# Retention attention and a Strassen feed-forward block in float32: weight rounding dealt out step by step, two evictions on ScalarE, sums of x^T kept in DRAM, a denser start

## The chip, the cores and the metric

The kernel runs on one core of a Trainium2 chip. The time is device microseconds of one execution, and the kernel before took 1169.26 us (median of 3 runs, 1168.03 to 1170.57). Five engines work from queues of their own, each in order: TensorE (PE in the profile, its weight loads PEld), VectorE (DVE), ScalarE (ACT), GpSimd (POOL) and SyncE (SP), which here issues nearly all DMAs. An instruction whose input isn't ready holds up everything behind it on its engine.

## The reference

```python
scores = scale * np.matmul(q, k.transpose(0, 1, 3, 2))          # q, k, v: (8, 8, 576, 64) float32
Dmat = np.where(rel >= 0, gamma[:, None, None] ** rel[None, :, :], 0.0)
attn = np.matmul(scores * Dmat[None], v)                        # no softmax: a decay per head instead
x = np.ascontiguousarray(attn.transpose(0, 2, 1, 3)).reshape(B * S, H * D)     # (4608, 512)
h = x @ w_in                                                    # w_in (512, 2048), float64
sp = np.maximum(h, 0.0) + np.log1p(np.exp(-np.abs(h)))
out = (h * erf(sp)) @ w_out                                     # w_out (2048, 512), float64
```

The weights come as float64; the kernel reads both 32-bit words of each and builds a float32 from them itself.

## The kernel before, in words

**Work units.** The 4608 tokens are cut into 9 chunks of 512 columns of x^T, and the 2048 columns of w_in into 4 groups g of 512. A slice n = 9g + c is one group on one chunk; there are 36. Each slice has a `First` (h = x w_in, then softplus and erf) and a `Second` (the product with w_out, added to an output sum o). Each is one level of Strassen's scheme in Winograd's form: seven products in place of eight. First n computes A11 A12 | S2 S3 S1 | S4 A22 (`first`, `middle`, `last`), Second n computes B11 B21 | T2 T3 T1 | B22 T4. One product is four float32 matmuls of 128x128x256; the trace shows each of them as two, so a product is a row "x8". All products of one half add into the same PSUM tile `a` one after the other (the partial sums): before the next product may add to it, the present sum must have been copied out. `t` (t1, t2) holds h, `s` its softplus, erf and sums, `g` and `e` are two further PSUM tiles, which First and Second share.

**Sums.** Strassen needs sums of the left and right operands. Those of the weights are made once for each group, four for `wa` (w_in) and four for `wb` (w_out), by `sums_in` and `sums_out` (L150, L156). Those of x^T are made for each slice by `sums_x` (L351) on VectorE into a tile `xs`: 4 sums for each of the 36 slices. Chunk c of x^T is written to DRAM (`xd`, 1 MB) when attention has made it, and read back by `load_x` for groups 1 to 3.

**Rounding.** A group has 8 weight parts, four of `wa` and four of `wb`, 512 KB each, in the raw tiles `wraw`. `round_weights` (L173) does one whole part at a call: two instructions on ScalarE, four on VectorE (L191, L194, L197, L201), two on GpSimd (L202, L203), then the load of the part four further on, and after the fourth part of `wa` or `wb` the four sums. It is called at seven places in the start, once behind First 0 and then once at the end of each Second (L566), so that a fourth part comes in every fourth slice.

**Attention** goes in 40 pieces of 128 (or 64) tokens, each in stages `transposes`, `scores`, `outputs`. The stages of chunk 0 come first; those of later chunks are dealt out one behind each product of group 0 (`run`, `attend`). `transposes(i)` also starts the loads of piece i+2 (three raw buffers).

**Order.** The program is written out by hand in the loop at L543: First n: S2 S3 S1, then Second n-1: B11 B21, First n: S4 A22, Second n-1: T2 T3 T1, First n+1: A11 A12, Second n-1: B22 T4, and so on. Each engine runs its instructions in that order. Behind S2 and S1, VectorE copies the partial sum out (L396, L401); behind A11 and S4 ScalarE does (L386, L407). At L545 to L548 the output sum o of Second n-1 (1 MB, `od`) and x^T of slice n+1 are loaded; in the last slice but one, o's load stands behind the stores (L573).

Of the kernel before, what the change touches and what calls it, by code (L numbers as in the profile page):

```python
# [11 lines left out]
FP32 = mybir.dt.float32  # L12
UINT8 = mybir.dt.uint8
UINT32 = mybir.dt.uint32
# [4 lines left out]
P = 128  # L19
# [27 lines left out]
def kernel(  # L47
# [69 lines left out]
    gk = gk.rearrange("p (s h) -> p s h", s=NS)  # L117
    gq = gq.rearrange("p (a i) -> p a i", a=NP)
    load(1)

# [26 lines left out]

    def sums_in(a11, s3, a12, a22, s1, s2, s4):  # L150
        tt(s1, s3, a22, ALU.add)
        tt(s2, s1, a11, ALU.subtract)
        tt(s3, a11, s3, ALU.subtract)
        tt(s4, a12, s2, ALU.subtract)

    def sums_out(b11, t3, b21, b22, t1, t2, t4):  # L156
        tt(t1, t3, b11, ALU.subtract)
        tt(t2, b22, t1, ALU.subtract)
        tt(t3, b22, t3, ALU.subtract)
        tt(t4, b21, t2, ALU.subtract)  # L160

    coming = parts()
    words = []
    rounded = [0]

    def load_weights():
        part = next(coming, None)
# [2 lines left out]
            nc.sync.dma_start(out=t[:, :].rearrange("p (h f) -> p h f", h=2), in_=part[0])  # L170
            words.append((t, *part[1:]))

    def round_weights():  # L173


        if not words:
            return
        t, name, g, slot, j, sums = words.pop(0)
        rounded[0] += 1
        w = operands(name, g)  # L180
        dst = w[:, slot : slot + 2, j, :]
        pairs = t[:, :].rearrange("p (h f two) -> p h f two", h=2, two=2)
        pairs_f = t[:, :].bitcast(FP32).rearrange("p (h f two) -> p h f two", h=2, two=2)
        low, high = pairs[:, :, :, 0], pairs[:, :, :, 1]
        r_f, high_f = pairs_f[:, :, :, 0], pairs_f[:, :, :, 1]
        a_f, a = dst, dst.bitcast(UINT32)
        nc.scalar.activation(a_f, high_f, AF.Abs)
        nc.scalar.mul(out=r_f, in_=low, mul=2.0**-52)


        nc.vector.tensor_scalar(  # L191
            out=a_f, in0=a_f, scalar1=HIGH_LEAST, scalar2=HIGH_MOST, op0=ALU.max, op1=ALU.min
        )
        nc.vector.tensor_scalar(  # L194
            out=a, in0=a, scalar1=3, scalar2=0x3FFFFFFF, op0=ALU.logical_shift_left, op1=ALU.bitwise_and
        )
        nc.vector.scalar_tensor_tensor(  # L197
            out=a, in0=high, scalar=0xC0000000, in1=a, op0=ALU.bitwise_and, op1=ALU.bitwise_or
        )

        nc.vector.tensor_scalar(out=high, in0=a, scalar1=0xFF800000, scalar2=None, op0=ALU.bitwise_and)  # L201
        nc.gpsimd.tensor_tensor(out=r_f, in0=high_f, in1=r_f, op=ALU.mult)  # L202
        nc.gpsimd.tensor_tensor(out=a_f, in0=a_f, in1=r_f, op=ALU.add)  # L203
        load_weights()
        if sums:
            sums(*(w[:, i] for i in range(7)))

    for _ in range(4):
        load_weights()

    ident = cpool.tile([P, P], FP32, name="ident")
    make_identity(nc, ident)
# [3 lines left out]
        nc.vector.memset(t, 0.0)  # L216


    x = {}
    live = {}  # L220
    kept = {}

# [37 lines left out]
    def outputs(i):  # L260
# [44 lines left out]
        while t0 < b * S + s0 + n:  # L305
            c = t0 // TCH
            if (0, c) not in x:
                x[0, c] = xpool.tile([P, n_dc, TCH], FP32, tag="x", name="x")
# [13 lines left out]
            t0 += m  # L322
            if t0 == (c + 1) * TCH:
                nc.sync.dma_start(out=xd[c], in_=x[0, c])

    stages = [(transposes, 0), (scores, 0)]
    for i in range(len(pieces)):
# [17 lines left out]


    def load_x(g, c):
        x[g, c] = xpool.tile([P, n_dc, TCH], FP32, tag="x", name="x")
        nc.sync.dma_start(out=x[g, c], in_=xd[c])

    def sums_x(g, c):  # L351
        t = x[g, c]
        s = xpool.tile([P, 4, 2, TH], FP32, tag="xs", name="xs")
        b11, b12, b21, b22 = (t[:, 2 * d : 2 * d + 2, h * TH : (h + 1) * TH] for d in range(2) for h in range(2))
        t1, t2, t3, t4 = (s[:, j] for j in range(4))
        tt(t1, b12, b11, ALU.subtract)
        tt(t2, b22, t1, ALU.subtract)
        tt(t3, b22, b12, ALU.subtract)
        tt(t4, b21, t2, ALU.subtract)
        x[g, c] = {A11: b11, A12: b21, S4: b22, A22: t4, S1: t1, S2: t2, S3: t3}  # L360

    class First:

# [40 lines left out]

# [122 lines left out]
    sums_x(0, 0)  # L527

    def run(steps):

        for _ in steps:
            attend(done[0] + 1)

    run(firsts[0].first())
    run(firsts[0].middle())
    run(firsts[0].last())
    firsts[0].erf()
    round_weights()
    attend(stages_for(2 * TCH))
    sums_x(0, 1)  # L540
    run(firsts[1].first())
    firsts[0].multiply()
    for b, nxt in zip(blocks[1:], blocks[2:] + [None]):  # L543
        n = order.index((b.g, b.c))
        if isinstance(b, First):  # L545
            seconds[n - 1].begin()
            if n + 1 < n_s and order[n + 1][0] > 0:
                load_x(*order[n + 1])  # L548
            run(b.middle())
            firsts[n - 1].sums()  # L550
            run(seconds[n - 1].first())
            run(b.last())
        elif n + 2 < n_s:
            f = firsts[n + 1]
            steps = b.middle()
            for step, _ in enumerate(steps):
                attend(done[0] + 1)
# [4 lines left out]
            sums_x(*order[n + 2])  # L562
            run(nxt.first())
            f.multiply()
            run(b.last())
            round_weights()  # L566
        elif n + 1 < n_s:
            firsts[n + 1].erf()
            run(b.middle())
            run(b.last())  # L570
            firsts[n + 1].multiply()
            firsts[n + 1].sums()
            seconds[n + 1].begin()  # L573
            run(nxt.first())
        else:
            run(b.middle())
            run(b.last())
# [30 lines left out]
```

## Time and profile before

| | |
|---|---|
| median of 3 runs | 1169.26 us |
| the profiled execution | 1166.91 us, its span 1165.1 us |
| busy: PE, DVE, ACT, POOL | 1082.6, 736.1, 372.1, 120.0 us |
| DMA | 150.27 MB, 40.2% of 16 engines |
| mean granted TensorE clock | 0.974 of 2.4 GHz |

TensorE is busy for 93% of the span, and the other engines for less than two thirds. What matters is what stands in the gaps of TensorE, and how the clock goes behind them. A time of an instruction is its start from the beginning of the span; "[5.11 <-DVE t L396]" behind a row says that its engine stood idle for 5.11 us before it, and which instruction ended the wait.

### The profile page before, as it was taken

How to read it: one execution, taken by the hardware profiler on the slowest of the kernel's cores; microseconds unless marked ns; L12 is line 12 of the kernel's file. 1: busy time of each engine (PE TensorE's matmuls, PEld its weight loads, DVE VectorE, ACT ScalarE, POOL GpSimd, SP SyncE). 2: the span in 40 equal slices, each digit the busy share in tenths (PEclk: the TensorE clock that was granted, in tenths of full speed). 3: DMA queues.
4: the chain of work that ended last, by engine and by line, in shares of the span. 5: the costliest groups of instructions: out<-in, count | busy, mean ns of one | idle time of the engine just before them, and what ended most of it. 6: DMA issues, size and time to landing. Idle time of an engine off the chain costs nothing. (4 is left out here: it accounts for less than half of the span.)

```text
span 1165.1 us, 15647 instructions
## 1 busy us (share of the span) xinstructions
PE 1082.6 (93%) x6400; PEld 922.7 (79%) x6400; DVE 736.1 (63%) x1240; ACT 372.1 (32%) x467; POOL 120.0 (10%) x110
## 2 busy tenths in 40 slices
PE   6679999999999998998999799989998999999996
PEld 5457888888788887876878688868887888888885
DVE  5756566666576575766566566666775565665654
ACT  3231433424314233333333333424332224322340
POOL 3411111111111000011000000000000000000000
PEclk8888999999999999999999899999999999999998
DMA  9546454554554122343234424332232442234422
GB/s 229 143 128 137 100 137 136 132 136 134 139 127 114 73 91 91 132 158 153 100 136 151 158 105 173 127 126 109 109 136 80 167 159 109 109 113 167 154 73 108
DMA packets 141127, 150.27 MB, mean 129 GB/s; under 512 B 115200, under 2 KB 115200, under 8 KB 132992
## 3 DMA queue, kind: packets, MB, share of 16 engines
q1 hardware_dynamic: 140912, 148.92, 40.2%
q8 instruction: 50, 0.82, 0.3%
q10 hardware_dynamic: 144, 0.36, 0.1%
q14 instruction: 21, 0.17, 0.0%
HBM read 102.07 MB, written 47.19 MB: 128 GB/s over the span
## 5 line engine op out<-in xcount | busy, mean ns | idle before, releaser
L450 PE MATMUL a<-wb,s 128*128 128x256 f32 x864 | 208.1, 384 | 10.8 <-DVE o L91 10.8
L450 PEld LDWEIGHTS a<-wb,s 128*128 128x128 f32 x864 | 162.7, 191 | 37.2 <-DVE o L91 12.6
L371 PE MATMUL a<-xs,wa 128*128 128x256 f32 x576 | 147.4, 401 | 32.9 <-DVE t L396 31.4
L407 ACT COPY t<-a 128x512 f32<-128x512 f32 x36 | 21.1, 585 | 435.3 <-PE a L371 420.4
L91 DVE TENSOR_TENSOR o<-a,o 128x512 f32<-128x512 f32 x108 | 74.4, 689 | 134.8 <-PE a L450 104.2
L371 PEld LDWEIGHTS a<-xs,wa 128*128 128x128 f32 x576 | 112.0, 199 | 56.1 <-DVE t L396 38.6
L371 PE MATMUL a<-x,wa 128*128 128x256 f32 x576 | 137.3, 381 | 0.0
L371 PE MATMUL g<-xs,wa 128*128 128x256 f32 x576 | 137.1, 381 | 0.0
L371 PEld LDWEIGHTS g<-xs,wa 128*128 128x128 f32 x576 | 108.2, 190 | 14.9
L371 PEld LDWEIGHTS a<-x,wa 128*128 128x128 f32 x576 | 108.1, 190 | 15.0
L202 POOL TENSOR_TENSOR wraw<-wraw 128x512 f32<-128x512 f32 x32 | 34.9, 1090 | 530.0 <-issue 425.6
L91 DVE TENSOR_TENSOR t<-t,s 128x1024 f32<-128x1024 f32 x72 | 85.9, 1234 | 0.0
L413 ACT ACTIVATE s<-t 128x1024 f32<-128x1024 f32 x72 | 72.1, 1048 | 36.1 <-DVE t L91 36.1
L91 DVE TENSOR_TENSOR t<-g,t 128x512 f32<-128x512 f32 x72 | 49.7, 690 | 43.9 <-PE g L371 42.6
L401 DVE COPY t<-a 128x512 f32<-128x512 f32 x36 | 24.9, 690 | 79.9 <-PE a L371 79.9
L418 ACT ACTIVATE s<-s 128x1024 f32<-128x1024 f32 x72 | 72.1, 1049 | 0.4
L450 PE MATMUL a<-wb,t 128*128 128x256 f32 x288 | 70.3, 388 | 1.9 <-DVE t L91 1.9
L371 PE MATMUL e<-x,wa 128*128 128x256 f32 x288 | 68.8, 382 | 0.0
L450 PE MATMUL g<-wb,s 128*128 128x256 f32 x288 | 68.6, 381 | 0.0
L450 PE MATMUL g<-wb,t 128*128 128x256 f32 x288 | 68.6, 381 | 0.0
L450 PE MATMUL e<-wb,t 128*128 128x256 f32 x288 | 68.4, 380 | 0.0
L228 POOL TENSOR_TENSOR raw_v<-raw_v,cst 128x512 f32<-128x512 f32 (+1 forms) x40 | 43.3, 1082 | 223.3 <-DMA raw_v<-in_v_dram 210.9
(61 smaller groups left out, 1435.3 us busy)
## 6 DMA issues: line engine op xcount, KB each, us to landing
od<-o SPq DMA_DIRECT2D x54, 512.0 KB, 3.1
x<-xd SPq DMA_DIRECT2D x27, 1024.0 KB, 8.9
o<-od SPq DMA_DIRECT2D x27, 1024.0 KB, 7.1
xd<-x SPq DMA_DIRECT2D x9, 1024.0 KB, 5.2
out_dram<-o SPq DMA_DIRECT2D x18, 512.0 KB, 3.0
raw_q<-in_q_dram SPq DMA_DIRECT2D x32, 256.0 KB, 4.8
raw_k<-in_k_dram SPq DMA_DIRECT2D x32, 256.0 KB, 3.9
raw_v<-in_v_dram SPq DMA_DIRECT2D x32, 256.0 KB, 4.0
```

The source lines that it names most:

```text
L91: nc.vector.tensor_tensor(out=out, in0=in0, in1=in1, op=op)
L202: nc.gpsimd.tensor_tensor(out=r_f, in0=high_f, in1=r_f, op=ALU.mult)
L228: nc.gpsimd.tensor_tensor(out=t[:n], in0=t[:n], in1=gk[:n, s0 // P, :].unsqueeze(2).to_broadcast([n, H, D]), op=ALU.mult,)
L371: nc.tensor.matmul(acc[:, j * TH : (j + 1) * TH], lhsT=weights["wa", self.g][:, a, d, j * P : (j + 1) * P], rhs=x[self.g, self.c][a][:, d, :],
L401: nc.vector.tensor_copy(out=self.t2[:, 1], in_=self.a)
L407: nc.scalar.copy(out=self.t2[:, 0], in_=self.a)
L413: nc.scalar.activation(self.s[:, j], t, AF.Softplus)
L418: nc.scalar.activation(self.s[:, j], self.s[:, j], AF.Erf)
L450: nc.tensor.matmul(acc[:, tp, :], lhsT=left[:, j * TH + tp * P : j * TH + (tp + 1) * P], rhs=weights["wb", self.g][:, b, j, :], start=(sta ...
```

## The change

`rounding` is now a generator that yields behind each step: the two ScalarE instructions, each of the first three VectorE instructions, the fourth with the GpSimd pair and the next load, and each sum of the weights. `round_weights(n)` takes n steps, and `run` deals them out behind named products: six in a slice (behind S2, S3, B11, B21, A11, T4). `most_g` keeps a group's rounding from starting before the tile that it overwrites is free. The copies behind S2 and S1 are on ScalarE. The sums of x^T are made once for each chunk, in group 0 (S3 in place of b12, the other three in three further columns of the tile x), and the whole tile, 1.75 MB for 1 MB, goes to DRAM and comes back; `xs` is gone. Raw buffers are four, and pieces are loaded three ahead. In the start, two rounding steps follow each attention stage and two stages follow each product of First 0; only `wa` is rounded ahead of First 0, and `wb` while First 0 and 1 run. The od load of the last slice moves ahead of the products of the one before.

```diff
-    raw = ctx.enter_context(tc.tile_pool(name="raw", bufs=3))
+    raw = ctx.enter_context(tc.tile_pool(name="raw", bufs=4))
-    xd = [dram.tile([P, n_dc, TCH], FP32, tag="xd", name="xd") for _ in range(n_ch)]
+    xd = [dram.tile([P, n_dc + 3, TCH], FP32, tag="xd", name="xd") for _ in range(n_ch)]
...
     def sums_in(a11, s3, a12, a22, s1, s2, s4):
         tt(s1, s3, a22, ALU.add)
+        yield
         tt(s2, s1, a11, ALU.subtract)
+        yield
...
-    def round_weights():
+    def rounding():
+        while words:
+            while words[0][2] > most_g[0]:
+                yield
...
+            nc.scalar.activation(a_f, high_f, AF.Abs)
+            nc.scalar.mul(out=r_f, in_=low, mul=2.0**-52)
+            yield
...
+            nc.vector.tensor_scalar(out=high, in0=a, scalar1=0xFF800000, scalar2=None, op0=ALU.bitwise_and)
+            nc.gpsimd.tensor_tensor(out=r_f, in0=high_f, in1=r_f, op=ALU.mult)
+            nc.gpsimd.tensor_tensor(out=a_f, in0=a_f, in1=r_f, op=ALU.add)
+            load_weights()
+            yield
+            if sums:
+                yield from sums(*(w[:, i] for i in range(7)))
+    def round_weights(n=1):
+        for _ in range(n):
+            next(round_step, None)
...
-        load(i + 2)
+        load(i + 3)
...
-    def sums_x(g, c):
+    def operands_x(g, c):
         t = x[g, c]
-        s = xpool.tile([P, 4, 2, TH], FP32, tag="xs", name="xs")
...
+        t1, t2, t4 = (t[:, n_dc + j, :].rearrange("p (d i) -> p d i", d=2) for j in range(3))
+        if g == 0:
+            tt(t1, b12, b11, ALU.subtract)
+            tt(t2, b22, t1, ALU.subtract)
+            tt(b12, b22, b12, ALU.subtract)
+            tt(t4, b21, t2, ALU.subtract)
+            nc.sync.dma_start(out=xd[c], in_=t)
...
             self.product(S2, self.a, False)
-            nc.vector.tensor_copy(out=self.t1[:, 1], in_=self.a)
+            nc.scalar.copy(out=self.t1[:, 1], in_=self.a)
...
             self.product(S1, self.a, False)
-            nc.vector.tensor_copy(out=self.t2[:, 1], in_=self.a)
+            nc.scalar.copy(out=self.t2[:, 1], in_=self.a)
...
-        if done[0] % 2 == 1 and rounded[0] < 7:
-            round_weights()
+        if done[0] >= 2:
+            round_weights(2)
...
+    run(firsts[0].first(), (0, 1), 2)
+    run(firsts[0].middle(), (0, 1, 2), 2)
+    run(firsts[0].last(), (0, 1), 2)
     firsts[0].erf()
...
         if isinstance(b, First):
+            most_g[0] = order[n - 1][0] + 1
             seconds[n - 1].begin()
...
-            run(b.middle())
+            run(b.middle(), (0, 1))
             firsts[n - 1].sums()
-            run(seconds[n - 1].first())
+            if n == 1:
+                round_weights(9)
+            run(seconds[n - 1].first(), (0, 1))
             run(b.last())
...
-            run(b.last())
-            round_weights()
+            run(b.last(), (1,))
         elif n + 1 < n_s:
             firsts[n + 1].erf()
+            seconds[n + 1].begin()
```

First place: VectorE in slice 17 before, from the last eviction of one Second into the next First. `wb` and `wraw` are the weights that are rounded, `t_4401` and `t_4445` the h of this slice, `s` the sums of the last slice's h, and L396 is the copy that S1 waits for.

```order
583 L91 TENSOR_TENSOR o<-g_4376,o 128x2x256
584 L191 TENSOR_SCALAR wb<-wb 128x2x256
585 L194 TENSOR_SCALAR wb<-wb 128x2x256
586 L197 SCALAR_TENSOR_TENSOR wb<-wraw,wb 128x2x256
587 L201 TENSOR_SCALAR wraw<-wb 128x512
588 L91 TENSOR_TENSOR wb<-wb 128x512 x4
589 L396 COPY t_4401<-a_4399 128x512
590 L401 COPY t_4445<-a_4399 128x512
591 L91 TENSOR_TENSOR t_4445<-g_4444,t_4445 128x512
592 L91 TENSOR_TENSOR s<-t_4331 128x512
```

The same slice in the changed kernel (`t_4381` is its h): three rounding steps are left here, and the sums of `wb` come one at a time.

```order
513 L91 TENSOR_TENSOR o<-g_4329,o 128x2x256
514 L205 TENSOR_SCALAR wb<-wb 128x2x256
515 L209 SCALAR_TENSOR_TENSOR wb<-wraw,wb 128x2x256
516 L214 TENSOR_SCALAR wraw<-wb 128x512
517 L91 TENSOR_TENSOR t_4381<-g_4380,t_4381 128x512
518 L91 TENSOR_TENSOR s<-t_4275 128x512
519 L91 TENSOR_TENSOR s<-s,t_4242 128x512
520 L91 TENSOR_TENSOR s<-t_4242,t_4275 128x512
521 L91 TENSOR_TENSOR s<-t_4242,s 128x512
522 L91 TENSOR_TENSOR o<-a_4407,o 128x2x256
523 L91 TENSOR_TENSOR wb<-wb 128x512
524 L91 TENSOR_TENSOR o<-e_4408,o 128x2x256
```

The two copies are gone from VectorE, and the first sum of the weights moved from straight behind the last rounding step to the seventh instruction behind it.

Second place: VectorE in the start. `sT` are the masked scores of an attention piece, `x` its output; before, the four sums of `wa` stand ahead of the third piece's `sT`.

```order
22 L191 TENSOR_SCALAR wa<-wa 128x2x256
23 L194 TENSOR_SCALAR wa<-wa 128x2x256
24 L197 SCALAR_TENSOR_TENSOR wa<-wraw,wa 128x2x256
25 L201 TENSOR_SCALAR wraw<-wa 128x512
26 L91 TENSOR_TENSOR wa<-wa 128x512 x4
27 L91 TENSOR_TENSOR sT<-s_330,cst 128x512
28 L91 TENSOR_TENSOR sT<-s_331,cst 128x512
```

And now, for the same piece and the rounding of the third part around it, and then First 1 and Second 0, where the rounding of `wb` ends (`t_900` is the h of slice 1, `s` the sums of slice 0's h):

```order
18 L201 TENSOR_SCALAR wa<-wa 128x2x256
19 L91 TENSOR_TENSOR sT<-s_315,cst 128x512
20 L91 TENSOR_TENSOR sT<-s_316,cst 128x512
21 L205 TENSOR_SCALAR wa<-wa 128x2x256
22 L209 SCALAR_TENSOR_TENSOR wa<-wraw,wa 128x2x256
...
86 L91 TENSOR_TENSOR t_900<-g_899,t_900 128x512
87 L91 TENSOR_TENSOR s<-t_547 128x512
88 L91 TENSOR_TENSOR s<-s,t_466 128x512
89 L91 TENSOR_TENSOR s<-t_466,t_547 128x512
90 L91 TENSOR_TENSOR s<-t_466,s 128x512
91 L214 TENSOR_SCALAR wraw<-wb 128x512
92 L91 TENSOR_TENSOR wb<-wb 128x512 x4
```

The third piece's scores moved ahead of most of the rounding, and the last rounding step and the sums of group 0's `wb` moved from ahead of First 1 to a place behind the sums of slice 0's h.

Third place: SyncE in a slice with rounding, before and then now. `od<-o` are the stores of one Second, `o<-od` the load for the next.

```order
184 L506 DMA od<-o 128x1024 x2
185 L170 DMA wraw<-in_moe_w_in_dram 128x2x512
186 L444 DMA o<-od 128x2048
187 L349 DMA x<-xd 128x2048
188 L506 DMA od<-o 128x1024 x2
```

```order
178 L529 DMA od<-o 128x1024 x2
179 L467 DMA o<-od 128x2048
180 L371 DMA x<-xd 128x3584
181 L179 DMA wraw<-in_moe_w_in_dram 128x2x512
182 L529 DMA od<-o 128x1024 x2
```

The load of raw weights moved from ahead of the loads of o and x to behind them, and the load of x has 3584 columns in place of 2048.

## Rows read from the trace of the kernel before

**Rows 1.** Windows: start:end length, busy (count) by engine, clock, DMA share, GB/s.

```profile
0.00:100.00 100.00, 66.94 (x594) 55.00 (x594) 57.29 (x111) 30.02 (x49) 32.29 (x33) 0.85 0.68 161
100.00:397.00 297.00, 294.57 (x2554) 244.24 (x2553) 196.39 (x403) 94.40 (x146) 44.99 (x42) 1.00 0.49 125
417.00:905.00 488.00, 451.24 (x2017) 387.95 (x2017) 314.09 (x480) 161.38 (x182) 42.26 (x36) 0.98 0.34 127
905.00:1129.00 224.00, 224.00 (x1039) 197.20 (x1038) 140.97 (x205) 69.68 (x72) 0.00 (x0) 1.00 0.36 133
```

**Rows 2.** Waits of TensorE, whole span: who waited for whom, total us, times, longest.

```profile
PE a L371 <- DVE t L396: 31.4, 17, 5.5
PE o L266 <- DVE sT L91: 15.1, 6, 9.2
PE a L450 <- DVE o L91: 10.8, 9, 2.0
```

**Rows 3.** Timeline (start, length, instruction): S1 of slices 8, 26 and 27.

```profile
417.04 1.99 PE L371 MATMUL a<-xs,wa 128*128 128x256 f32 x8
...
905.01 1.89 PE L371 MATMUL a<-xs,wa 128*128 128x256 f32 x8
...
929.19 1.89 PE L371 MATMUL a<-xs,wa 128*128 128x256 f32 x8
```

**Rows 4.** Timeline of slice 17, where a fourth part is rounded.

```profile
656.48 1.89 PE L371 MATMUL a<-xs,wa 128*128 128x256 f32 x8
...
659.35 0.43 DVE L201 TENSOR_SCALAR wraw<-wb 128x512 uint32<-128x512 uint32 x1
...
661.35 1.28 POOL L203 TENSOR_TENSOR wb<-wb,wraw 128x512 f32<-128x512 f32 x1
662.65 0.56 SPq L170 DMA_DIRECT2D wraw<-in_moe_w_in_dram  x1
662.66 1.90 DVE L91 TENSOR_TENSOR wb<-wb 128x512 f32<-128x512 f32 x3 [2.29 <-POOL wb L203]
...
664.48 0.68 DVE L396 COPY t<-a 128x512 f32<-128x512 f32 x1
...
665.21 3.78 PE L371 MATMUL a<-xs,wa 128*128 128x256 f32 x8 [5.11 <-DVE t L396]
```

**Rows 5.** Timeline of slice 14: VectorE's first eviction of o.

```profile
590.35 0.69 DVE L91 TENSOR_TENSOR o<-a,o 128x512 f32<-128x512 f32 x1 [3.80 <-DMA o<-od]
```

**Rows 6.** Groups of instructions by form: count, busy us, mean ns, idle before.

```profile
L396 DVE COPY t<-a 128x512 f32<-128x512 f32 x36 | 24.7, 685 | 6.2 <-PE a L371 6.2
...
L407 ACT COPY t<-a 128x512 f32<-128x512 f32 x36 | 21.1, 585 | 435.3 <-PE a L371 420.4 <-DVE o L91 15.0
```

**Rows 7.** Timeline of the start: third piece, A11 of First 0 and 1, B21 of Second 0.

```profile
38.02 2.47 PE L266 MATMUL o<-sT,raw_v 128*64 128x128 f32 x16 [9.15 <-DVE sT L91]
...
49.34 1.99 PE L371 MATMUL a<-x,wa 128*128 128x256 f32 x8
...
100.60 1.99 PE L371 MATMUL a<-x,wa 128*128 128x256 f32 x8
...
118.20 1.99 PE L450 MATMUL e<-wb,t 128*128 128x256 f32 x8
```

**Rows 8.** DMA issues, 900 to 1000 us: count, KB each, median us from issue to landing.

```profile
o<-od SPq DMA_DIRECT2D x4, 1024.0 KB, 7.8
x<-xd SPq DMA_DIRECT2D x4, 1024.0 KB, 9.9
```

**Rows 9.** Timeline of slice 26: x is issued, and the A11 that needs it.

```profile
904.01 1.15 SPq L349 DMA_DIRECT2D x<-xd  x1
...
918.83 1.89 PE L371 MATMUL a<-x,wa 128*128 128x256 f32 x8
```

**Rows 10.** Timeline of the last slice.

```profile
1147.86 0.69 DVE L91 TENSOR_TENSOR o<-a,o 128x512 f32<-128x512 f32 x1 [1.15 <-DMA o<-od]
...
1148.69 3.65 PE L450 MATMUL a<-wb,s 128*128 128x256 f32 x8 [2.01 <-DVE o L91]
```

More of the change, by code (lines that the diff above doesn't have):

```diff
@@ L119 @@
     load(1)
+    load(2)
     A11, S3, A12, A22, S1, S2, S4 = range(7)
@@ L151, in sums_in @@
         tt(s1, s3, a22, ALU.add)
+        yield
         tt(s2, s1, a11, ALU.subtract)
+        yield
         tt(s3, a11, s3, ALU.subtract)
+        yield
         tt(s4, a12, s2, ALU.subtract)
+        yield
     def sums_out(b11, t3, b21, b22, t1, t2, t4):
         tt(t1, t3, b11, ALU.subtract)
+        yield
         tt(t2, b22, t1, ALU.subtract)
+        yield
         tt(t3, b22, t3, ALU.subtract)
+        yield
         tt(t4, b21, t2, ALU.subtract)
+        yield
     coming = parts()
     words = []
-    rounded = [0]
+    most_g = [1]
     def load_weights():
@@ L171, in load_weights @@
             words.append((t, *part[1:]))
-    def round_weights():
[L176 to L206, printed above, removed]
@@ new lines, in rounding @@
+    def rounding():
+        while words:
+            while words[0][2] > most_g[0]:
+                yield
+            t, name, g, slot, j, sums = words.pop(0)
+            w = operands(name, g)
+            dst = w[:, slot : slot + 2, j, :]
+            pairs = t[:, :].rearrange("p (h f two) -> p h f two", h=2, two=2)
+            pairs_f = t[:, :].bitcast(FP32).rearrange("p (h f two) -> p h f two", h=2, two=2)
+            low, high = pairs[:, :, :, 0], pairs[:, :, :, 1]
+            r_f, high_f = pairs_f[:, :, :, 0], pairs_f[:, :, :, 1]
+            a_f, a = dst, dst.bitcast(UINT32)
+            nc.scalar.activation(a_f, high_f, AF.Abs)
+            nc.scalar.mul(out=r_f, in_=low, mul=2.0**-52)
+            yield
+            nc.vector.tensor_scalar(
+                out=a_f, in0=a_f, scalar1=HIGH_LEAST, scalar2=HIGH_MOST, op0=ALU.max, op1=ALU.min
+            )
+            yield
+            nc.vector.tensor_scalar(
+                out=a, in0=a, scalar1=3, scalar2=0x3FFFFFFF, op0=ALU.logical_shift_left, op1=ALU.bitwise_and
+            )
+            yield
+            nc.vector.scalar_tensor_tensor(
+                out=a, in0=high, scalar=0xC0000000, in1=a, op0=ALU.bitwise_and, op1=ALU.bitwise_or
+            )
+            yield
+            nc.vector.tensor_scalar(out=high, in0=a, scalar1=0xFF800000, scalar2=None, op0=ALU.bitwise_and)
+            nc.gpsimd.tensor_tensor(out=r_f, in0=high_f, in1=r_f, op=ALU.mult)
+            nc.gpsimd.tensor_tensor(out=a_f, in0=a_f, in1=r_f, op=ALU.add)
+            load_weights()
+            yield
+            if sums:
+                yield from sums(*(w[:, i] for i in range(7)))
@@ L219, with x_tile @@
     x = {}
+    def x_tile():
+        return xpool.tile([P, n_dc + 3, TCH], FP32, tag="x", name="x")
     live = {}
@@ L347, in load_x @@
     def load_x(g, c):
-        x[g, c] = xpool.tile([P, n_dc, TCH], FP32, tag="x", name="x")
+        x[g, c] = x_tile()
         nc.sync.dma_start(out=x[g, c], in_=xd[c])
-    def sums_x(g, c):
+    def operands_x(g, c):
         t = x[g, c]
-        s = xpool.tile([P, 4, 2, TH], FP32, tag="xs", name="xs")
         b11, b12, b21, b22 = (t[:, 2 * d : 2 * d + 2, h * TH : (h + 1) * TH] for d in range(2) for h in range(2))
[L355 to L360, printed above, removed]
+        t1, t2, t4 = (t[:, n_dc + j, :].rearrange("p (d i) -> p d i", d=2) for j in range(3))
[5 more added lines that the diff above has]
+            nc.sync.dma_start(out=xd[c], in_=t)
+        x[g, c] = {A11: b11, A12: b21, S4: b22, A22: t4, S1: t1, S2: t2, S3: b12}
     class First:
@@ L524, with run @@
         attend(done[0] + 1)
-        if done[0] % 2 == 1 and rounded[0] < 7:
-            round_weights()
[L527 to L536, printed above, removed]
+        if done[0] >= 2:
+            round_weights(2)
+    operands_x(0, 0)
+    most = [stages_for(2 * TCH) - 1]
+    def run(steps, rounds=(), stages=1):
+        for step, _ in enumerate(steps):
+            attend(min(done[0] + stages, most[0]))
+            if step in rounds:
+                round_weights()
+    run(firsts[0].first(), (0, 1), 2)
+    run(firsts[0].middle(), (0, 1, 2), 2)
+    run(firsts[0].last(), (0, 1), 2)
     firsts[0].erf()
-    round_weights()
+    most[0] = stages_for(3 * TCH) - 1
     attend(stages_for(2 * TCH))
-    sums_x(0, 1)
-    run(firsts[1].first())
+    operands_x(0, 1)
+    round_weights(4)
+    run(firsts[1].first(), (0, 1))
     firsts[0].multiply()
+    round_weights(4)
     for b, nxt in zip(blocks[1:], blocks[2:] + [None]):
@@ L548 @@
                 load_x(*order[n + 1])
-            run(b.middle())
+            run(b.middle(), (0, 1))
             firsts[n - 1].sums()
-            run(seconds[n - 1].first())
+            if n == 1:
+                round_weights(9)
+            run(seconds[n - 1].first(), (0, 1))
             run(b.last())
+            most[0] = stages_for(min((n + 3) * TCH, n_tok)) - (n + 3 < n_ch)
         elif n + 2 < n_s:
             f = firsts[n + 1]
-            steps = b.middle()
-            for step, _ in enumerate(steps):
-                attend(done[0] + 1)
+            for step, _ in enumerate(b.middle()):
+                attend(min(done[0] + 1, most[0]))
                 if step == 0:
@@ L561 @@
                 attend(stages_for((n + 3) * TCH))
-            sums_x(*order[n + 2])
-            run(nxt.first())
+            operands_x(*order[n + 2])
+            run(nxt.first(), (0,))
             f.multiply()
-            run(b.last())
-            round_weights()
+            run(b.last(), (1,))
         elif n + 1 < n_s:
             firsts[n + 1].erf()
+            seconds[n + 1].begin()
             run(b.middle())
```

6 lines of the change are left out of this document (2 added, 4 removed).

## The prediction

> **What bounds the kernel now.** I read the windows first. From 100 to 397 us, with attention beside the products, TensorE is busy for 294.57 of 297 us at a granted clock of 1.00: nothing is to be had there. In the first 100 us it is busy for 67 us at 0.85, and from 417 to 905 us for 451 of 488 at 0.98 [rows 1]. So two stretches lose time. The waits of TensorE name the reasons: 31.4 us for the VectorE copy behind S2 (L396), 15.1 us for the masked scores of attention, 10.8 us for evictions of o [rows 2].
>
> How much the second stretch loses is read from S1, which comes once in a slice. From slice 26 to 27, when nothing is rounded any more, it takes 929.19 - 905.01 = 24.18 us, and TensorE is busy for all of the 224 us behind 905 us [rows 1]. From slice 8 to 26 it takes 905.01 - 417.04 = 487.97 us; 18 slices of 24.18 are 435.24. The loss is 52.7 us [rows 3].
>
> One slice shows the mechanism. In slice 17 S2 starts at 656.48; its copy could run one product, 1.7 us, later. VectorE, however, has the last rounding step at 659.35, then a sum that needs GpSimd's product, which ends at 661.35 + 1.28 = 662.63. Three sums follow, the copy starts at 664.48, and S1 at 665.21, 5.11 us late. It then takes 3.78 us where it takes 1.99 elsewhere, so the clock fell to the lower level during the wait [rows 3, 4]. A fourth part comes five times in that stretch (slices 9, 13, 17, 21, 25), and five waits of this size are most of the 31.4 us; the longest is 5.5 us [rows 2]. The evictions of o have another reason: SyncE holds the raw-weight load until GpSimd is done (662.65), and o's load stands behind it, so VectorE waits 3.80 us for o [rows 4, 5].
>
> **The change part by part, and its sum.**
>
> *Copies on ScalarE, rounding in steps, the raw load behind the others.* The copy takes 0.585 us on ScalarE for 0.685 on VectorE [rows 6], and it stands there behind the copy after A11 and at most two rounding instructions, all of which are ready long before. The six steps of a slice, starting in slices 10 and 19 (`most_g`), make 24 steps of a fourth part fall on exactly four slices. The last rounding step then lies behind S3 and the first sum behind B11, with the sums of h between, so GpSimd has two products and more for the 2.85 us that it needs (from 659.35 + 0.43 to 662.63) [rows 4]. What is late next? S3 needs the eviction behind T4, and T3 the one behind A22; each has one product of 1.7 us of room, no rounding step directly ahead of it, and a VectorE that lost the two copies and, from slice 9 on, four sums of x^T. I count the whole 52.7 us as won; at worst half of it, 26 us, stays (rival 2).
>
> *A larger x.* 27 loads of 1.75 MB for 1 MB. In slice 26 x is issued at 904.01, lands 9.9 us later at 913.9, and A11 needs it at 918.83 [rows 8, 9]: 4.9 us of room. o's load is issued just ahead of x's and lands in 7.8 us, x in 9.9 [rows 8], so x's 1.05 MB need at least 2.1 us behind o and at most, if the issues lie 0.7 us apart (an estimate: the raw load's issue takes 0.56 us [rows 4]), 2.8; 0.79 MB more are 1.6 to 2.1 us. Cost 0, cover 2.8 us; the upper end is rival 3, the lower end nothing, since an x that comes earlier frees nobody. The Trainium skill ("DMA: Bandwidth & Descriptors", Queues, rings and completion order) has each DMA engine take the descriptors of one ring in order, yet calls completion not FIFO per issuing engine; by the first half the term is nothing, by the second o could land late and the evictions behind B11 with it. The rows, x landing behind o by about what its bytes take, go with the first half.
>
> *The start.* (a) The third piece's scores no longer stand behind the whole rounding of `wa` and its four sums. That wait was 9.15 us [rows 7]. Walking VectorE's new order I get A11 of First 0 at about 38 for 49.3, an estimate: the whole wait and 2 us of the whole parts of `wb` that before stood between the later pieces. (The first piece's scores also come earlier, but the second piece still waits on ScalarE for the first raw weights, which now land behind the third piece's q, k, v; I count nothing.) (b) First 0 with its attention lasted 49.34 to 100.60 us, 51.3 us. From 100 to 397 us TensorE does 91 products; at 24.18 / 14 = 1.73 us each they leave 137 us for 30.5 pieces, 4.5 us a piece [rows 1, 3]. Seven products and 4.7 pieces are 33 us; I add 6 for a wait of the fifth (half) piece's scores behind the last sums of `wa` and the sums of x. So A11 of First 1 comes at about 77 to 78, 23 us early. (c) New: `wb` is now ready late. Between what VectorE does at A11 of First 1 and the last rounding step of `wb` stand 41 instructions (outputs and sums of x, scaling and sums of h, nine rounding steps, scores); at 196.39 / 403 = 0.49 us each [rows 1] that is 20 us, and GpSimd needs 2.85 more. B21, which needs that part, stands 118.20 - 100.60 = 17.6 us behind A11 on TensorE [rows 7]. It waits some 5.3 us, and the clock falls as in slice 17: 1.8 more [rows 4]. Net 23 - 7 = 16 us. Bounds: only (a)'s 9.15 less the 7, so 2 us; and 30 us without (c) and the 6. I take 16, from the walk.
>
> *Attention in group 0.* The windows leave 2.4 us of waits there to be won [rows 1]; VectorE now carries group 1's rounding beside scores and evictions in smaller steps, and SyncE's store of x waits for four sums. I set the 2 against the 2: 0, between -2 and +6.
>
> *The end.* In the last slice VectorE waits 1.15 us for o, and T2, 2.01 us late, runs at the lower clock (3.65 us) [rows 10]. With o there early, the sums of h still come first: 1.5 us won, between 0 and 3.
>
> Sum: 52.7 + 16 + 0 + 1.5 = 70.2 us. The profiled execution took 1166.91 us (span 1165.1 and 1.8 around it): 1096.7. The median of the runs is 2.35 us above that execution, so 1099.
>
> **Rivals.** 1. *The start gives all it can.* First 1's A11 early by 30 us, and B21 not late: for it, the fourth part's rounding might run while VectorE waits for TensorE; against it, VectorE works strictly in order, and scaled h needs erf first. 1099 - 14 = 1085.
>
> 2. *The stalls are moved, not removed.* A step waits for ScalarE or GpSimd ahead of the eviction behind A22 or T2, each with 1.7 us of room, in half of the 16 rounding slices. For it: VectorE is busy 314 of 488 us [rows 1], and every step waits on another engine. Against it: the steps' inputs are a product old. Half of 52.7 stays: 1125. The Trainium skill ("TensorE: Matmul & The Clock Gate", A second HAM failure mode: psum-queue depth-cycling) tells of a PE that is short of work for a moment between groups, again and again, and loses clock by it; by that rule this rival would cost more. The stretch from 100 to 397 us has 2.4 us of waits and a clock of 1.00, so here the short ones cost only themselves.
>
> 3. *x lands late; slower than before.* If a load's whole time grows with its size, x lands 9.9 x 1.75 = 17.3 us after its issue, at 921.3, and A11 waits 2.5 us in 27 slices: 67 us. With a clock that falls each time (3.78 for 1.99) it is 48 more: 1099 + 115 = 1214. It decides from a landing 14.8 us behind the issue; to undo the gain of 70 us, 2.6 us per slice are needed without the clock, or 0.8 with it. Against it: the 9.9 us are mostly the queue behind stores and o, which don't grow.
>
> 4. *Nothing gained*: the copies were late because evictions come late anyhow. Against it, slices 26 on, with the same copies on VectorE, have no wait. 1169.
>
> **How the numbers follow.** Forecast 0.68 (own range 1088 to 1112), rival 1 0.12, rival 2 0.13, rival 3 0.05 (it ends above the old time in four cases of five), rival 4 0.02. The range 1080 to 1125 takes in the start's bounds and half of rival 2. A measurement of this kernel tells about 0.2%, 2.3 us, from no change; faster 0.94, same 0.02, slower 0.04.
>
> **What would show it.** The waits of TensorE should hold no copy behind S2 above a microsecond in total, S1 to S1 should be 24.2 us from slice 9 on, rounding or not, and the clock 1.00 there. A11 of First 1 should start near 78 us and B21 of Second 0 be the longest wait of the run after the first piece, ended by `wb`. x should land about 12 us after its issue. The forecast is wrong if x is named as releaser of A11, if the S1 distance stays above 25 us in rounding slices, or if First 1 starts after 90 us.

## The result, and the profile after

The changed kernel takes 1098.78 us (median of 4 runs, 1098.42 to 1099.44) and the kernel before, beside it, 1169.91 us: a ratio of 0.939 (95% interval 0.937 to 0.941). The forecast was 1099. One execution of all that stand in this document, the profiled one of the raw load alone (below), took 2824.89 us where the three others of its kernel took 1158.58 to 1161.44; its time and its trace are left out. The changed kernel's profiled execution took 1099.01 us with a span of 1097.2, 67.9 less than before's 1165.1. These are its windows, with the columns of [rows 1].

```profile
0.00:100.00 100.00, 81.74 (x728) 67.75 (x728) 60.55 (x130) 35.44 (x60) 31.16 (x33) 0.91 0.84 196
100.00:397.00 297.00, 293.18 (x2479) 243.25 (x2479) 189.89 (x386) 107.57 (x164) 49.27 (x44) 0.99 0.50 136
417.00:905.00 488.00, 488.00 (x2263) 429.60 (x2262) 264.14 (x399) 201.13 (x239) 37.23 (x32) 1.00 0.47 173
```

Beside [rows 1]: from 417 to 905 us TensorE went from 451.24 busy of 488 to 488.00, at a clock of 1.00 for 0.98; in the first 100 us from 66.94 to 81.74; from 100 to 397 it lost 1.4. Its waits, whole span, as [rows 2]:

```profile
PE s L278 <- ACT kT L269: 5.1, 2, 4.5
PE o L290 <- DVE sT L91: 4.4, 4, 2.6
PE e L473 <- POOL wb L216: 3.8, 1, 3.8
PE a L473 <- DVE t L91: 1.9, 1, 1.9
...
PE a L473 <- DVE o L91: 1.6, 2, 0.8
```

The 31.4 us behind the copy of S2 and the 10.8 us behind o's eviction are gone (1.6 us of the latter stand in the last slices). S1 of slices 8, 26 and 27, as [rows 3]:

```profile
404.37 1.89 PE L394 MATMUL a<-x,wa 128*128 128x256 f32 x8
...
839.49 1.89 PE L394 MATMUL a<-x,wa 128*128 128x256 f32 x8
...
863.66 1.89 PE L394 MATMUL a<-x,wa 128*128 128x256 f32 x8
```

From 8 to 26 that is 435.12 us, 24.17 a slice, for 487.97 before: 52.85 us won. S1 of slice 8 comes 12.7 us earlier (417.04), and from S1 of slice 26 to the end of the span it is 257.7 us for 260.1. 52.85 + 12.7 + 2.4 = 67.9. Slice 17, where [rows 4] had the stall:

```profile
619.82 0.69 DVE L209 SCALAR_TENSOR_TENSOR wb<-wraw,wb 128x512 uint32<-128x512 uint32 x1
619.93 0.58 SPq L467 DMA_DIRECT2D o<-od  x1
620.20 1.89 PE L394 MATMUL g<-x,wa 128*128 128x256 f32 x8
620.40 0.59 ACT L419 COPY t<-a 128x512 f32<-128x512 f32 x1 [6.32 <-PE a L394]
...
621.93 1.89 PE L394 MATMUL a<-x,wa 128*128 128x256 f32 x8
622.23 1.28 POOL L216 TENSOR_TENSOR wb<-wb,wraw 128x512 f32<-128x512 f32 x1
623.54 0.55 SPq L179 DMA_DIRECT2D wraw<-in_moe_w_in_dram  x1
```

The copy (L419) starts 0.2 us behind S3 (620.20), on an engine that waited for S2, and S1 follows S3 by 1.73 us. The raw load still waits for GpSimd, but o's load went out 3.6 us ahead of it.

### The profile page after: what moved, and what is told of

Its sections match the earlier page's. It is cut to its first block, busy times and chain, and to the rows that moved or that the text cites. A ratio compares the mean times of both kernels' runs of the same rounds, so it can differ in the third digit from the quotient of the medians.

```text
span 1097.2 us, 15487 instructions
## 1 busy us (share of the span) xinstructions
PE 1067.0 (97%) x6400; PEld 918.6 (84%) x6400; DVE 618.7 (56%) x1060; ACT 413.2 (38%) x539; POOL 120.3 (11%) x110
## 4 chain that ended last, share of the span: by engine, by line
PE 90%; DVE 0%; issue 0%
PE a L473 23%; PE a L394 22%; PE g L473 11%; PE g L394 11%; PE e L473 6%; PE e L394 5%; PE s L278 3%; PE o L290 2%; PE o L300 2%; PE kv L312 1%; PE pt_q L267 1%; PE pt_k L267 1%; DVE o L91 0%; DVE t L91 0%
## 5 line engine op out<-in xcount | busy, mean ns | idle before, releaser
L394 PE MATMUL a<-x,wa 128*128 128x256 f32 x1152 | 276.9, 383 | 0.0
L394 PEld LDWEIGHTS a<-x,wa 128*128 128x128 f32 x1152 | 218.0, 191 | 30.9 <-issue 0.4
L473 PE MATMUL a<-wb,s 128*128 128x256 f32 x864 | 205.8, 381 | 1.6 <-DVE o L91 1.6
L394 PE MATMUL g<-x,wa 128*128 128x256 f32 x576 | 137.2, 381 | 0.0
L394 PEld LDWEIGHTS g<-x,wa 128*128 128x128 f32 x576 | 108.2, 190 | 14.8
L419 ACT COPY t<-a 128x512 f32<-128x512 f32 x36 | 21.1, 585 | 195.7 <-PE a L394 195.7
L430 ACT COPY t<-a 128x512 f32<-128x512 f32 x36 | 21.1, 586 | 151.2 <-PE a L394 151.2
L473 PEld LDWEIGHTS e<-wb,t 128*128 128x128 f32 x288 | 55.3, 194 | 12.0 <-POOL wb L216 4.2
L473 PEld LDWEIGHTS a<-wb,t 128*128 128x128 f32 x288 | 54.5, 192 | 9.9 <-DVE t L91 2.3
## 6 DMA issues: line engine op xcount, KB each, us to landing
x<-xd SPq DMA_DIRECT2D x27, 1792.0 KB, 10.8
```

The costliest lines, as they stand in the source:

```text
L394: nc.tensor.matmul(acc[:, j * TH : (j + 1) * TH], lhsT=weights["wa", self.g][:, a, d, j * P : (j + 1) * P], rhs=x[self.g, self.c][a][:, d, :],
L419: nc.scalar.copy(out=self.t1[:, 1], in_=self.a)
L473: nc.tensor.matmul(acc[:, tp, :], lhsT=left[:, j * TH + tp * P : j * TH + (tp + 1) * P], rhs=weights["wb", self.g][:, b, j, :], start=(sta ...
```

## The experiments

Two theories stood against each other. *Queue order*: TensorE was late because a copy stood in VectorE's queue behind an instruction that waited for GpSimd, and o's load in SyncE's queue behind one that did. *Load*: VectorE had too much to do in a slice. "Stretch" below is from 417 to 905 us; before, TensorE was busy there for 451.24 us and VectorE for 314.09 [rows 1]. A kernel that loses less puts more slices into these 488 us, so work is compared over the 18 slices from S1 of slice 8 to S1 of slice 26.

**The copies alone** (kernel before; the same for S1):

```diff
-            nc.vector.tensor_copy(out=self.t1[:, 1], in_=self.a)
+            nc.scalar.copy(out=self.t1[:, 1], in_=self.a)
```

> The kernel before with one edit: the copies behind S2 and S1 run on ScalarE. Theory (the steady stretch loses time because the copy behind S2 stands in VectorE's queue behind sums that wait for GpSimd): the copy-behind-S2 wait of TensorE (31.4 us) and the low clock behind it go, with nothing else changed; 40 to 48 of the 52.7 us between slice 8 and 26 are won, S1 to S1 over these 18 slices falls from 488.0 to 440 to 448 us, time about 1122 to 1130. The waits for o's eviction behind B11 (10.8 us) stay, since SyncE still holds the raw load ahead of o's load. Rival (VectorE has too much work in a slice, and any product that needs it comes late): the wait moves to the next eviction, at most half of the 52.7 is won, time 1143 or more.

1132.52 us, ratio 0.968 (0.967 to 0.970). From S1 of slice 8 to S1 of 26 it took 453.5 us: 34.5 of the 52.7 are won, fewer than the theory asked for, more than the rival. No wait for a copy behind S2 is left in the stretch, but one row grew (waits of TensorE, then the timeline of one slice):

```profile
PE a L450 <- DVE o L91: 17.0, 14, 2.4
```

```profile
567.63 0.55 SPq L170 DMA_DIRECT2D wraw<-in_moe_w_in_dram  x1
568.27 0.55 SPq L444 DMA_DIRECT2D o<-od  x1
...
575.47 0.69 DVE L91 TENSOR_TENSOR o<-a,o 128x512 f32<-128x512 f32 x1 [4.48 <-DMA o<-od]
576.22 1.99 PE L450 MATMUL a<-wb,s 128*128 128x256 f32 x8 [2.20 <-DVE o L91]
```

It was 10.8 us before [rows 2]. In the kernel before, the late copy hid part of the late o: with S1 on time, o's eviction is due sooner and o's load is not.

**The raw load alone, and both** (kernel before; from slice 8 on, where the first x is read back, not from slice 2 as the expectation says):

```diff
-        load_weights()
+        if late[0]:
+            owed[0] += 1
+        else:
+            load_weights()
...
                 load_x(*order[n + 1])
+                late[0] = True
+                while owed[0]:
+                    owed[0] -= 1
+                    load_weights()
```

> The kernel before with one edit: from slice 2 on the load of raw weights is issued behind the loads of o and x instead of ahead of them. The copies alone won 34.5 of the 52.7 us between slice 8 and 26 and left waits for o's eviction. Theory (two queues, each with its own stall): the evictions of o no longer wait for o, the 10.8 us of that wait go and nothing else does, the copy-behind-S2 waits of about 5 us in every fourth slice stay: 1155 to 1162. Rival (the o waits come from VectorE's rounding and not from SyncE's order): no change, 1167 or more.

1158.58 to 1161.44 us, ratio 0.994 (0.992 to 0.996): 7 us less, a time within the theory's range. Without a trace, that the waits for the copy stayed isn't shown.

> The kernel before with two edits: copies behind S2 and S1 on ScalarE, and the raw load behind the loads of o and x. Rounding still in whole parts, sums of x^T in every slice, start as before. Theory: these two queue orders are the whole loss of the steady stretch; S1 to S1 over the 18 slices from 8 to 26 falls to 435 to 440 us, time 1115 to 1121, so that dealing the rounding out and keeping the sums of x^T add nothing there. Rival: whole parts and 4 sums in each slice still fill VectorE too far ahead of an eviction; 8 us or more stay (as the 8 us that sums of x^T in every slice cost the changed kernel), 1123 or more.

1112.51 us, ratio 0.953 (0.952 to 0.955), below the theory's range; from S1 of slice 8 to S1 of 26 it took 435.69 us, which is in it. The stretch from 417 to 905 us, and those 18 slices:

```profile
417.00:905.00 488.00, 487.97 (x2260) 428.97 (x2259) 319.51 (x486) 200.87 (x239) 42.80 (x36) 1.00 0.39 142
417.41:853.10 435.69, 435.66 (x2018) 382.91 (x2016) 290.71 (x444) 182.45 (x218) 42.40 (x36) 1.00 0.39 142
```

No wait is left, with the rounding in whole parts and the sums of x^T in every slice. That VectorE is busy for 319.5 us of the stretch, more than the 314.1 before, doesn't yet speak against the load theory: for the same 18 slices it works 290.7 us, less than 314.1, since the copies have left it. But with the copies alone it had the same work there, 290.5 us, and 17.8 us more were lost. One edit saves 3.2% and the other 0.6%, both together 4.7%: the 0.9% more comes only with both.

**Copies back on VectorE** in the changed kernel (the first diff turned round):

> The changed kernel with one edit back: the copies behind S2 and S1 are on VectorE again. Theory (queue order): with the rounding dealt out in steps nothing that waits for GpSimd stands ahead of a copy, so the copies may stay on VectorE: 1099 to 1103, no wait for a copy above 1 us each. Rival (the copies had to leave VectorE for its load): 72 copies of 0.685 us back on VectorE bring waits back, 1115 or more.

1099.41 us, ratio 0.940 (0.938 to 0.942): the same as changed. In the stretch TensorE is again busy for 488.00 us. In the start one wait for a copy is left, which the theory had put below 1 us:

```profile
PE a L394 <- DVE t L419: 2.8, 1, 2.8
```

It is S1 of First 1 (97.28); B21 of Second 0 then waits 2.0 us for `wb` in place of 3.8. So in the stretch the rounding in steps and the copies on ScalarE each clear the copy's way, and the change does it twice.

**Sums of x^T in every slice** in the changed kernel, x of 1 MB:

```diff
-            tt(b12, b22, b12, ALU.subtract)
...
+        s = xpool.tile([P, 4, 2, TH], FP32, tag="xs", name="xs")
+        t1, t2, t3, t4 = (s[:, j] for j in range(4))
+        tt(t1, b12, b11, ALU.subtract)
...
```

> The changed kernel with one part undone: x^T goes to DRAM without its sums (1 MB), and the four sums are made on VectorE in every slice again. Theory: the sums never were on the path, they only fill VectorE; 1097 to 1102, and x lands about 1.5 us sooner after its issue than with 1.75 MB. Rival (VectorE's load counts): 27 x 4 sums of about 0.45 us, 49 us more of VectorE work, give waits in each slice, 1110 or more.

1105.77 us, ratio 0.946 (0.944 to 0.948): 7 us slower, which is neither answer. From S1 of slice 8 to S1 of 26 it took 443.24 us for 435.12, and 5.7 of these 8.1 us are four waits of one kind (waits of TensorE, then one of them in the timeline):

```profile
PE g L395 <- DVE o L91: 5.7, 4, 1.4
```

```profile
566.98 0.42 DVE L214 TENSOR_SCALAR wraw<-wb 128x512 uint32<-128x512 uint32 x1
...
567.53 1.04 POOL L215 TENSOR_TENSOR wraw<-wraw 128x512 f32<-128x512 f32 x1 [40.78 <-ACT wraw L197]
567.92 3.97 DVE L91 TENSOR_TENSOR t<-t,s 128x1024 f32<-128x1024 f32 x2
...
568.65 2.15 POOL L216 TENSOR_TENSOR wb<-wb,wraw 128x512 f32<-128x512 f32 x1
...
571.81 0.68 DVE L91 TENSOR_TENSOR o<-a,o 128x512 f32<-128x512 f32 x1
...
573.14 1.99 PE L395 MATMUL g<-xs,wa 128*128 128x256 f32 x8 [1.43 <-DVE o L91]
```

The scaling of h (`t<-t,s`, two instructions) takes 3.97 us, and GpSimd's second product 2.15. Behind 400 us the scaling takes 2.35 or 2.36 us in the 24 slices without GpSimd beside it and 3.96 to 3.97 in the 4 with it; GpSimd's second product takes 1.28 to 1.36 elsewhere. The 1.6 us more are more than the wait of 1.43. With the four sums of x^T ahead of it, the last rounding step (L214) comes 3.9 us behind the eviction behind T1 (563.12) where it comes 1.3 us behind it in the changed kernel (564.76 for 563.42), and so GpSimd's pair falls beside the scaling. In the changed kernel the pair of the same slice is nearly done when the scaling starts (567.72 for 567.56), and the scaling takes 2.38 us. The theory was right on x's landing in the stretch, 1.4 us sooner than the changed kernel's 10.9 (below):

```profile
x<-xd SPq DMA_DIRECT2D x20, 1024.0 KB, 9.5
```

**Only the steps left**: both copies on VectorE and the sums in every slice.

> The changed kernel with both copies back on VectorE and the sums of x^T made in every slice: of the steady stretch's edits only the rounding in steps, the order of the raw load and the four raw buffers are left. Theory (queue order): no copy waits, since nothing that waits for GpSimd stands ahead of one; S3's waits of 1.4 us for the eviction behind T4, seen with the sums in every slice, stay: 1104 to 1109. Rival (VectorE's load; its busy time in the stretch from 417 to 905 us would be some 345 of 488 us, more than before's 314): 1115 or more.

1108.03 us, ratio 0.947 (0.945 to 0.949), with the same row of waits (5.7, 4, 1.4), and again one wait for a copy, 2.8 us at S1 of First 1, which the theory had excluded. From S1 of slice 8 to S1 of 26:

```profile
405.57:848.79 443.22, 437.30 (x2017) 382.13 (x2016) 312.08 (x471) 160.20 (x180) 39.46 (x31) 1.00 0.38 138
```

VectorE does 312.1 us of work for these 18 slices, as before (314.1), and they take 443.2 us in place of 488.0. So 44.8 of the 52.85 us were won with VectorE's work unchanged: order, not load. Here the load theory falls. The other 8 us are the price of the sums in every slice once the rounding is in steps; with the rounding in whole parts (both orders mended, above) they cost no wait.

**The old start** in the changed kernel: whole parts, seven ahead of First 0, one stage behind each product.

```diff
-        if done[0] >= 2:
-            round_weights(2)
+        if done[0] % 2 == 1 and parts_done[0] < 7:
+            round_whole()
...
-    run(firsts[0].first(), (0, 1), 2)
+    run(firsts[0].first())
```

> The changed kernel with the start of before: whole parts of the rounding, seven of them ahead of First 0, one behind it, one attention stage behind each product; from slice 2 on as changed. Theory: the start's term of the sum, 16 us net, comes back: 1113 to 1118, A11 of First 1 again near 100 us and no wait for wb at B21 of Second 0. Rival 1: the start is worth little because its late wb gives the gain back, 1105 or less. Rival 2: it is worth more, 25 us or more, and the steady stretch correspondingly less than the 52.7 us.

1112.41 us, ratio 0.951 (0.949 to 0.954), and A11 of First 1 at 103.4, with no wait for `wb`. The start is worth 13.6 us by the medians, a little under the theory's range.

**One more load ahead of x** in the changed kernel, 1 MB into a spare tile:

```diff
+        nc.sync.dma_start(out=spare[0], in_=xd[c][:, :n_dc])
         nc.sync.dma_start(out=x[g, c], in_=xd[c])
```

> The changed kernel with one more load: in each of the 27 slices that read x back, 1 MB of the same DRAM tile goes into a spare tile that nobody reads, issued just ahead of x. Theory (x lands by its bytes): 2.1 to 2.8 us more for the added MB, x at 13 to 14 us behind its issue for 10.8 now, and 15.1 us are there before A11 (838.16 to 853.30): no wait, 1097 to 1102. Rival (the landing grows in proportion, as in the rival of a late x): 10.8 x 2.75 / 1.75 = 17 us, A11 waits some 2 us in 27 slices, 1150 or more.

1098.57 us, ratio 0.940 (0.938 to 0.942). DMA issues of the stretch with the spare load (the columns of [rows 8]):

```profile
x<-xd SPq DMA_DIRECT2D x20, 1792.0 KB, 12.3
...
o<-od SPq DMA_DIRECT2D x19, 1024.0 KB, 7.1
```

and of the changed kernel in the same stretch:

```profile
x<-xd SPq DMA_DIRECT2D x20, 1792.0 KB, 10.9
...
o<-od SPq DMA_DIRECT2D x19, 1024.0 KB, 7.2
```

x lands 1.4 us later behind its issue, and the issue comes later too, since the spare load's stands ahead of it. Issue and A11 in one slice with the spare load:

```profile
838.12 0.48 SPq L376 DMA_DIRECT2D x<-xd  x1
...
852.07 1.89 PE L399 MATMUL a<-x,wa 128*128 128x256 f32 x8
```

These are 13.95 us, for 15.14 in the changed kernel (838.16 to 853.30). So 1 MB more takes 2.6 us of the room, within what its bytes were put at (2.1 to 2.8) and far from the rival's 6 us. But it nearly uses up the room: the latest x lands 13.5 us behind its issue, half a microsecond ahead of its A11.

**A denser start.** First 0 with two rounding steps of `wb` behind each product, two in place of nine ahead of B21:

```diff
-    run(firsts[0].first(), (0, 1), 2)
-    run(firsts[0].middle(), (0, 1, 2), 2)
-    run(firsts[0].last(), (0, 1), 2)
+    run(firsts[0].first(), (0, 0, 1, 1), 2)
+    run(firsts[0].middle(), (0, 0, 1, 1, 2, 2), 2)
+    run(firsts[0].last(), (0, 0, 1, 1), 2)
...
-                round_weights(9)
+                round_weights(2)
```

> The changed kernel with wb of group 0 rounded more densely: two steps behind each product of First 0 and two in place of nine before B11 of Second 0. Theory (wb is late because its steps stand in VectorE's queue behind First 1's work, while VectorE has idle time in First 0): the 3.8 us wait of B21 and the lower clock behind it go, 3 to 6 us faster than the changed kernel, 1093 to 1096. Rival: the added steps come ahead of masked scores of attention in First 0 and take it back, 1098 to 1102.

1095.66 us, ratio 0.939 (0.938 to 0.941). The wait for `wb` is gone; the ratio alone doesn't set it apart from the changed kernel, which ran on another chip. The next version also begins the rounding one stage later:

```diff
-        if done[0] >= 2:
-            round_weights(2)
+        if done[0] >= 3:
+            round_weights(2 + 2 * (done[0] == 4))
```

> As the run with dense wb, and the rounding in chunk 0's attention starts one stage later, so that qT and kT of the second piece stand on ScalarE ahead of the first instruction that waits for raw weights (two steps are caught up one stage later). Theory: the 4.5 us wait of the second piece's scores goes; 3 to 4.5 us faster than dense wb alone, 1089 to 1093. Rival: what bounds the first 40 us is the arrival of raw weights and of q, k, v, so the later pieces or A11 of First 0 wait instead; within 1.5 us of dense wb alone.

1096.05 us, ratio 0.939 (0.937 to 0.941): no more than dense `wb`, so the rival's answer. The second piece's scores came at 13.53 (18.82 in the changed kernel), and the time went into the next wait, for a state copy that now stands behind the raw weights (TensorE):

```profile
18.19 0.71 PE L267 MATMUL pt_q<-ident,raw_q 128*128 128x128 f32 x4 [3.50 <-ACT state L324]
...
25.88 1.16 PE L278 MATMUL s<-qT,kT 64*128 64x128 f32 x16
```

The last row is the third piece's scores; in the changed kernel they came at 25.86. The profiled execution was nevertheless 5.4 us shorter, so I ran both on one chip:

> The changed kernel once more, unchanged, to stand beside the version with the denser and later start on one chip. 1096 to 1101.

> The version with dense wb and the rounding begun one stage later, once more, beside the changed kernel on one chip. If the 5.4 us by which its profiled span was shorter (1091.8 for 1097.2) belongs to the version: 1092 to 1095 with the changed kernel at 1096 to 1101, and a ratio interval below that of the changed kernel. Rival (the gain was one execution's): less than 2 us between the two.

The changed kernel took 1098.48 us (1097.04 to 1099.17), this version 1095.65 (1094.44 to 1096.41), 2.8 us less, which lies between the theory and the rival. Their runs don't overlap, though the intervals of the ratios to before do (0.937 to 0.941; 0.935 to 0.939), and the first run of the same version had a ratio of 0.939. So the gain rests on this one comparison, and what the later first step adds to dense `wb` isn't shown. The profiled execution shows a place of the gain:

```profile
100.00:397.00 297.00, 297.00 (x2504) 246.74 (x2503) 190.99 (x387) 108.41 (x165) 46.41 (x41) 0.99 0.50 135
```

TensorE has no gap there, for 293.17 us busy in the changed kernel beside it, where it waited 3.8 us for `wb`.

## Why the prediction was right

**The stretch with rounding, 52.7 us: right in size, half right in why.** 52.85 us were won, and the two mechanisms that the prediction read from slices 17 and 14 are enough for all of it: both orders mended alone take 435.69 us for the 18 slices, and the changed kernel 435.12. The prediction didn't divide the 52.7 us; 40 to 48 were then expected of the copies alone, whose row was the larger (31.4 for 10.8 us). They gave 34.5. The raw load alone gave 7 by the medians, so some 11 us came only with both: a part of the late load of o stood behind the copy's stall, where a table of waits can't show it. The prediction also counted three edits as one cure; the runs show that copies and steps are each enough for the copy, while every run without a wait in the stretch has the raw load behind o's.

**Larger x, 0: right.** DMA issues between 900 and 1000 us, for [rows 8]:

```profile
x<-xd SPq DMA_DIRECT2D x4, 1792.0 KB, 10.2
...
o<-od SPq DMA_DIRECT2D x4, 1024.0 KB, 6.7
```

x lands 10.2 us behind its issue, for 9.9 before and about 12 forecast. That window has four loads. Over the stretch it is 10.9 us (20 loads, above); before:

```profile
x<-xd SPq DMA_DIRECT2D x19, 1024.0 KB, 8.9
...
o<-od SPq DMA_DIRECT2D x17, 1024.0 KB, 7.1
```

That is 2.0 us more, as worked out (1.6 to 2.1); the forecast of 12 was too high because it started from the 9.9. The 4.9 us of room were read in one slice; in the changed kernel x lands at least 3.2 us ahead of its A11. Rival 3 is out: with still 1 MB more no A11 waits. The Trainium skill ("DMA: Bandwidth & Descriptors", Queues, rings and completion order) left room for a late o by its second half; o lands in 6.7 us for 7.8 (in the stretch 7.2 for 7.1), so the trace shows none of that.

**The start, 16 us: too large by 3.** Rows of the changed kernel, for [rows 7]: A11 of First 0, the fifth piece, A11 of First 1, B21 of Second 0 with the end of `wb`.

```profile
40.73 1.99 PE L394 MATMUL a<-x,wa 128*128 128x256 f32 x8
...
50.01 0.91 PE L290 MATMUL o<-sT,raw_v 64*64 64x64 f32 x16 [2.61 <-DVE sT L91]
...
54.75 3.45 PE L394 MATMUL a<-x,wa 128*128 128x256 f32 x8
...
82.78 1.99 PE L394 MATMUL a<-x,wa 128*128 128x256 f32 x8
...
101.60 1.13 PE L473 MATMUL e<-wb,t 128*128 128x256 f32 x4
...
105.22 1.27 POOL L216 TENSOR_TENSOR wb<-wb,wraw 128x512 f32<-128x512 f32 x1
...
106.55 2.07 PE L473 MATMUL e<-wb,t 128*128 128x256 f32 x4 [3.82 <-POOL wb L216]
```

A11 of First 0 was forecast for 38 and came at 40.73; First 0 took 42.05 us for 39, so A11 of First 1 came at 82.78 for 77 to 78: 17.8 us won, not 23. The walk took TensorE's steady pace, 1.73 us a product, for a stretch with the lower clock in it: S2 of First 0 (54.75) takes 3.45 us. The late `wb` was foreseen by place and size: 3.82 us for 5.3, and 2.07 us for the half product behind it, where the first half took 1.13. One sign came out otherwise: B21's is not the longest wait behind the first piece, since the second piece's scores wait 4.5 us for kT, which stands on ScalarE behind the first raw weights. S1 of slice 2 is 9.8 us early (147.79 for 157.59), S1 of slice 8 12.7: 2.9 us more were won in the attention stretch, forecast as 0 between -2 and +6. Part of that is the same attention at another place, so only the sum of the two, 12.7 for 16, compares.

**The end, 1.5 us: 2.4.** Rows of the last slice, from B11 to T2:

```profile
1077.45 2.97 PE L473 MATMUL a<-wb,t 128*128 128x256 f32 x8 [1.92 <-DVE t L91]
...
1080.50 0.68 DVE L91 TENSOR_TENSOR s<-t,s 128x512 f32<-128x512 f32 x1
1081.10 0.68 DVE L91 TENSOR_TENSOR o<-a,o 128x512 f32<-128x512 f32 x1
...
1082.69 1.89 PE L473 MATMUL a<-wb,s 128*128 128x256 f32 x8
```

T2 (1082.69) no longer waits, and runs in 1.89 us for 3.65 [rows 10]. The eviction of o that it needs (1081.10) follows straight on the last sum of h (1080.50), as the prediction said ("the sums of h still come first"). B11's wait of 1.92 us for the scaled h was there before as well:

```profile
1142.97 1.99 PE L450 MATMUL a<-wb,t 128*128 128x256 f32 x8 [1.91 <-DVE t L91]
```

Now the lower clock falls on B11 (2.97 us), where before it fell on T2. From B11 to T2 only 0.5 us are won (5.24 us for 5.72); the other 1.9 us lie behind T2's start, where the clock is no longer low. With both orders mended and o's last load at its old place the end is 1.6 us shorter, so how much of the 2.4 us that load's move gives isn't shown.

The sum was 70.2 where 67.9 came. The 0.2 us between forecast and median are luck: that execution was forecast at 1096.7 and took 1099.0, and the 2.35 us added for the median made up for it. Rival 2 (moved stalls) did not come in the changed kernel, but one of its kind lies 7 us away: without the sums kept in DRAM the step behind A11 meets the scaling of h. The prediction's condition for a higher price didn't arise: those four waits of 1.4 us, and with the copies alone one in each of slices 10 to 20 (0.33 to 2.40 us), leave the clock of the stretch at 1.00, though behind the longest T2 takes 3.67 us. So the rule on a TensorE that is short of work again and again ("TensorE: Matmul & The Clock Gate" of the Trainium skill, named in the prediction) has at most that one case here. Rival 1 had the right direction for `wb`; mending that, with the later first step, gave 2.8 us, not 14.

## What to carry to other kernels

Where an engine is late, read what stands ahead in its queue and what that waits for, before counting its busy time: the same VectorE work (312 and 314 us for 18 slices) took 443 us in one order and 488 in another. Compare work for the same slices, not for the same stretch of time, which holds more slices in the faster kernel. Two stalls in one slice can hide each other, so the row of a wait can be too low for what its cure is worth once the other is gone. Take out the queue orders one by one, and both; what is left tells which of the other edits are needed.

## What the runs showed of the hardware

VectorE and GpSimd don't run everything side by side. In the kernel with sums in every slice, the two scaling instructions take 2.35 us together alone and 3.96 to 3.97 beside two products on GpSimd, of which the second stretches from 1.28 to 2.15. The four cases repeat to 0.01 us, and again in the kernel with only the steps left. The Trainium skill ("SBUF — State Buffer", Who interferes with whom) has a VectorE instruction with two inputs in SBUF and a GpSimd instruction that reads SBUF contend for a pair of ports that is an exclusive lock. The rows fit the two engines taking turns: GpSimd's first product ends at 568.57, one scaling instruction of 1.2 us later its second can start, which then ends at 570.80, and the second scaling ends 1.1 us behind that. No run here moved that pair alone.

A load's landing grew by about what its added bytes were worked out to take, not in proportion to its size. 0.75 MB more moved x's landing in the stretch from 9.5 to 10.9 us (the kernel with sums in every slice against the changed one) and from 8.9 to 10.9 (before against changed), where 1.6 to 2.1 us were worked out. 1 MB more ahead of it took 2.6 us, 1.2 of them as a later issue, where 2.1 to 2.8 were expected.
